# Two of seven mixing products replaced by a second level of seven, over two pairs of token tiles

## The chip, the cores and the metric

The kernel runs on one core of a Trainium2 chip. The metric is the device time of one execution in microseconds: 230.19 us before the change, the median of 3 runs (229.83 to 230.55).

## The reference

One transformer block on 2048 tokens of width 512: linear attention, then a gated mixer whose spatial weight mixes all tokens. Random bf16 inputs; cut to what matters:

```python
x = A_x                                              # 1 x 2048 x 512
h = x + _A_ref(_layernorm(x), A_wqkv, A_wo)          # linear attention, 32 heads
h2 = h + _B_ref(_layernorm(h), B_w_in, B_w_sp, B_b_sp, B_w_out)

def _B_ref(x, w_in, w_sp, b_sp, w_out):              # F = 1792, Fh = 896
    z = _gelu(jnp.einsum('bsd,df->bsf', x, w_in))
    z1 = z[..., :Fh].copy()
    z2 = _layernorm(z[..., Fh:], axis=-1)
    g = jnp.einsum('ts,bsf->btf', w_sp, z2) + b_sp[None, :, None]
    return jnp.einsum('bsf,fd->bsd', z1 * g, w_out)
```

The change concerns the product of `w_sp` (2048 x 2048) with `z2` (2048 x 896).

## The kernel before

Tokens are cut into 16 tiles of 128. The stages follow one another and overlap at the edges: normalize x and transpose it; keys, queries and the linear attention; h and its normalized, transposed form `hnT`; the two halves of `w_in` (`z2`, normalized, and the gate partner `z1`); the mixing with `w_sp`; the output product with `w_out`.

From the `w_in` stage on, large products are done by Winograd's form of the Strassen scheme: each factor is cut in 2 x 2 blocks, and seven products of blocks and some block sums take the place of eight products. One such unit for `w_in` is a *cell* (two token tiles: `cell3` for z2, `cell2` for z1; each of its seven products is 2 matmuls of 128 x 448). One for `w_out` is `mo_pair` (L1048: products of 3 matmuls of 128 x 256, and two remainders of 512 columns).

The unit for the mixing is `mix(i, c)` (L995) on a *pair*: output tiles i and i + 8. `wt[n]` holds the transposed rows of `w_sp` for output tile n, 16 blocks of 128 x 128. The four weight blocks of a pair are `y11, y21` (the first and second eight blocks of `wt[i]`) and `y12, y22` (those of `wt[i+8]`); the blocks of z2 are the first and last eight token tiles by the columns 0 to 447 (`lo`) and 448 to 895 (`hi`). Each of the seven products is 8 matmuls of 128 x 448. Three PSUM banks hold the results: `A`, `B`, `E` (a set; pairs take turns at the sets 0, 1, 2 and 3, 4, 5; banks 6 and 7 belong to `cell2` and `mo_pair`). In order of the program text:

- m1 = y11 with z2 `lo` into A (L1002); ScalarE copies A to B (L1003)
- VectorE: `q1 = y12 + y22` (L1004); m5 = q1 with `zt1` into E (L1005)
- ScalarE takes E out into `p5` twice, with the bias (L1007)
- VectorE: `q2`, and two more row sums written in place over `y12` and `y11` (L1008 to 1010)
- m6 onto B, m2 onto A, copy of B to E, m3 onto E, m7 and m4 onto B (L1011 to 1020)
- after m2, m3, m7 and m4 VectorE adds, multiplies with z1 (`gate`, `gate_p`), and SyncE sends the gated tile through a transposing DMA into `zgT` (L1017, L1022), which `mo_pair` reads.

`zt1`, `zt2`, `zt4` are sums of z2 blocks made once (`t1_sums`, `t_sums`). The pairs come in the order `MIX = (0, 1, 2, 3, 7, 4, 5, 6)`. Four cells of z1 stand among the pairs (`Z1S`, L956, L1085): cells 2 and 6 after the first pair, 3 and 7 after the second.

What sets the order: each operation is recorded with the tiles that it reads and writes (`add`, L106). Dependences come from their addresses, for PSUM from whole banks (L73). `ORDER` (L16) is a packed list of operation numbers; taken engine by engine it is the fixed instruction order of each queue, and a wait is placed wherever an operation depends on another engine or a DMA (`emit`, L163). Nothing is reordered at run time, so an instruction that waits holds back all that stands behind it on its engine.

All weight tiles `wt` are loaded by transposing DMAs on SyncE's queue (`load_w`), two per tile. Tiles 4, 12, 5, 13, 6, 14 (`W4`, L1088) share memory with the sums `hs` and `ws` of the cells, so they can only be loaded when the last cell has read those.

`sa`, `p5`, `vs`, `us`, `tmp` are buffers for row sums, biased products and the sums of `mo_pair`; before the change `vs`, `us` and `tmp` lie where `hnT` was (`o_pk`), and a dummy matmul (L1090) orders them behind the last cell.

Of the kernel before, what the change touches and what calls it, by code (L numbers as in the profile page):

```python
# [6 lines left out]
FP32 = mybir.dt.float32  # L7
# [4 lines left out]
P = 128  # L12
GRAN = 16
EARLY = 0
SEM_NS = 45.0
ORDER = "c-jrpg8~@j0tV0z|7_c~ZQHhOw_44tc{SU%QA5qPS6j`h*4DPRd!ON)Scr|d0EqaAgXBmFBOQbkNRNObNQH<fh6pH%49JKyh=<}xi!4Zh)F^?HNQkT`g-j@ovdE0=sD*5(gSIG#D9C}j$c5UdhcZZnoG6d>$c+j}jQYrf{K$)TsE7{eh<s>(0;q&eXox~+jDo0)LFkM|Xo4h&jsX~mu4sxc&<s`41<g?fg)ta4&>ht<8A(wcU!ogoVj_B=1-`=9n1YsQg`PNqNf?4;n2KJQhC^71p@@nZ=#4)327NIdtuYL3FdWOV0wb^rt1%uwV<x`GNQ}Z^tid>}#X9uEFBpwkn1KG6gQNHX8!;Q3@GaJ31Lop5V&FT>!znDrd_=+`9K#qa!C0KYX)Hx#Y{nLx#2;9Ot$2uC*oNKMjy+g_g?NPhIDozQ5&Q5H&f*{*;|$JW2X^8-uHXVL;|4C`Dz4!YZXzb0;1;gqC7$9}+{P>1!9CnXWd4R|c!3RkjVSyR&#;DT`5YVh7veA~|3ggP$KQy{7<_<__y_A4oxdX<qwx(s{lCIHB;>zH%C~qAGZEu6Hk0u)K0u7c<Rk-=Fe0-v2MaI)3o-#CF(=EgBy%wp6SELgGdEK(9m}#5YcM5ivnJCs16MH(OS2A}GcEJ5F!M4qi?AH?u_(*46}xdIv#=O5F(d0TKP#{WTeBj2vO6oW7AvzQi?bf<vjlsv7ppNFzhoO`WdnZAZ}<;;^Dz5xJcsftwq;*7WOdGBI}YJ@Y|kp3z;F2@8?ghAa4vslKlbNrPUIX`<s>#`N6zCg4(BiYiEnv_T{xe&c#OAsh)3Cs$9b2(@*PKT0T=QFf8#+8;39TqW8ULQuIFOj=L25gQ@-a#PG%>b;w3)gM^53t9LdXU!p(fn!}`F^yuxI9LFfx!r9>syRQ|_N%%>z8%+VZ6>oX%LseWgEjbTbH;W$RrKt@tf3Kh^a{=rW?%~YDsmpsGNimX@~#2=VOv2~W26-C#$l-F5Ag%n3|^^gTsN`;k0Gx&;GHIvy?LQ%Dx#S~4=R8p_mTm#ia15{M;lwIf8RHap1W%WJNY8h9srM57>a;S_Rv4zU%F%zhjHnF^JFr5bJD^*u|B~%9GR0XwGbPds9-DDeeRz+=P4Sk_5%BAznsG9ndnY4|S^cUwVx4P<UeW_aNrbK$e;rd3qG*p#UTMM*P!!%cUG)i@}TYs~PMrwriXr9_CvEFdB_9}*AYC9LHyT)je7HS9Esje0)ua;<^R&%V{>zXEOsn)22Zm5T@>!zw|ijHWR#%ZeRsi$tKmu~Bw)@q&ZXuNi^nwIOJrs)^$VsG8mdfn3mb<}k2=C}G)^|e7W^qc<G3T@PPy01-Ypq2VwKj?S;p?|bloitNhG*Mf%hY$5YhxAx|v`UZkvsUYg`s$cY>ZqQopJu6{-U{BPy?m~He5MonsL$H27dox|Jgzf(ua}yw*E+xtqW7zjPN|6h(*>3AC!Ll2N`I=cF6x}@+Aiuj+M(dTRmcbQM*UUH#U06)bx9HYmm)isuPBCNI<^b@N1azmM|C{Maa>1n8ULjCPT)k2=!8z}22SGAj^?DU<4#WI<WA{wPT`uqs#N~P^<Bzoo!YgW#$|oPbsgR5T-hC*-WgrR8C>2KoXORk#T9+WSzXVKebAYm&4--bRbAaV+|ZqU!uNd49evVAeabm~#;4uLz1+mdoy&LK&0XBohyAm2`>b2JtGoN0&%1`d@d)?yNMG^=S8^Wbbu(XaK40`@_i<~t^)-L*fBe=xeAPpI)4%$<o4cJyxwqRmzkl<65A`iS@Ie3Juie7K{m66N*T4IrAA7X>`H7!-ko)_oUwD`c_y^DSbHDOS|LcN&=W%}R_a5vIUgy8v(qsIm2lz|3_eB5YkN#wY|NPkuF~e9-_ZObz%?=@Ah#daU6=r$7qlCC2LWmt^c&_7xSRqn~9-@T_jvqF8o)d?J;kIWwPFU{*AyG&YrZ{<+?1i4{ubeSt4oSl_rwrfvjW;-1ND~%0bx09Xg{)zXvxRgaeaIBPbIGvQ*+Y(yGc5KpZ*-Qh)wx5ikSEOd4lj59P%z{TMMB}Q(yN>=6bOaFHm`8;P&zDesj%G(yxLn_CKL;0L%Fcm4MX{`&pTZqR1OtGrBEdt@P6-djIi5P!wnY=)x%Qnam~;;Gz!(ikFF7#gxcXJ*9mn))KDv=4JAU;&@9vs^+JQtJoF4LLd(!Pv<iJfo6sw?4ShrV&@prgokP3OA!G=hLjTY`bPK)1fG{xh3tdBx@IT`6A!q"  # L16


class _Op:
# [233 lines left out]
def bass_sequential_preLN__linear_attn_block__mixer_gmlp__prompt_kernel(  # L253
# [30 lines left out]
    def take(n):  # L284
# [57 lines left out]
          for c, os in enumerate(((o_sp + 5 * ZR, o_win + KD * FH * 2), (o_win + KD * FH * 2 + S, o_win + KD * FH * 2 + 2 * S)))]  # L342
# [1 line left out]
    p5z = [g.sbuf(f"p5z{c}", o_wo + c * ZR, [HW], FP32) for c in (0, 1)]  # L344
    u_t = [g.sbuf(f"u{c}", o_sp + 4 * ZR + c * HW * 2, [HW], BF16) for c in (0, 1)]
    V3 = HF * D
    vs = [g.sbuf(f"vs{k}", o_pk + k * V3, [HF, D // 2], BF16) for k in range(4)]
    us = [[g.sbuf(f"us{c}{k}", o_pk + 4 * V3 + (4 * c + k) * HF * P * 2, [HF, P], BF16) for k in range(4)] for c in (0, 1)]
    tmp = [[g.sbuf(f"tmp{c}{k}", o_pk + 4 * V3 + 8 * HF * P * 2 + (2 * c + k) * 2 * D, [D // 2], FP32) for k in (0, 1)]
           for c in (0, 1)]  # L350
    wout = g.sbuf("wout", o_wout, [KF, D], BF16)
    ct = g.sbuf("ct", o_ct, [KD, D], BF16)
    m = g.sbuf("m", o_m, [KD, D], BF16)
# [51 lines left out]
    def matmuls(out_ap, pairs, start=True, stop=True, onto=False, **k):  # L405
        n = out_ap.free_size() if callable(getattr(out_ap, "free_size", None)) else out_ap.shape[-1]

        kw = {"skip_group_check": True} if onto else {}

        def fn(pe):  # L410
            inst = None
            for i, (a, b) in enumerate(pairs):
                inst = pe.matmul(out_ap, lhsT=a, rhs=b, start=start and i == 0, stop=stop and i == len(pairs) - 1, **kw)  # L413
            return inst
        return PE(fn, [a for p in pairs for a in p], [out_ap], len(pairs) * max(65.0, n / 2.4 + 2.5), **k)
# [7 lines left out]
    def act(out_ap, in_ap, func, n, bias=None, scale=None, extra=(), accum=None, **k):  # L423
        kw = {}
        if bias is not None:
            kw["bias"] = bias
        if scale is not None:
            kw["scale"] = scale
        if accum is not None:
            kw["accum_out"] = accum  # L430
        ps = in_ap.tensor.name == "psum"
        return g.add("ACT", lambda ac: ac.activation(out_ap, in_ap, func, **kw), [in_ap, *extra],  # L432
                     [out_ap] + ([accum] if accum is not None else []),
                     cost=act_cost(n, ps) + 93 * len(extra) + (92 if accum is not None else 0), lat=120, **k)
# [10 lines left out]
    def dma_t(out_ap, in_ap, name, issue=1310.0, lat=1600.0, **k):  # L445
        return g.add("SP", lambda q: q.dma_start_transpose(out_ap, in_ap), [in_ap], [out_ap], cost=issue, lat=lat,  # L446
                     dma=name, **k)
# [276 lines left out]
    def load_w(n):  # L724
        nonlocal late
        for j in (0, HT):
            op = dma_t(wt[n][:, j:j + HT, :], B_w_sp[n * P:(n + 1) * P, j * P:(j + HT) * P], f"wt{n}", issue=1350, lat=2900)
            op.soft.add(late.i)
            late = op
# [109 lines left out]
    def half(b):  # L839
        return bank(b, HW)  # L840
# [4 lines left out]
    def comb(out_ap, a, b, op):  # L845
        n = 1
        for s in out_ap.shape[1:]:
            n *= s
        return dve(lambda v: v.tensor_tensor(out_ap, a, b, op), [a, b], [out_ap], n, acc=2)  # L849
# [103 lines left out]

    SETS = (0, 3)
    Z1C = {1: (0,), 3: (1,), 5: (4,), 7: (5,)}
    Z1S = {0: (2, 6), 1: (3, 7)}  # L956
    HB = 2
    SQ = range(0, NT - 2, 2)
    w_sums(win2, wq1[1])
# [22 lines left out]
    def gate(n, c, b):  # L982
        o = z1[n][:, c]
        dve(lambda v: v.scalar_tensor_tensor(o, half(b), b32[:, n:n + 1], o, op0=ALU.add, op1=ALU.mult),  # L984
            [half(b), b32[:, n:n + 1], o], [o], HW, ps=True)
# [3 lines left out]
    def gate_p(n, c, b, p):  # L989
        o, u = z1[n][:, c], u_t[cnt[0] % 2]  # L990
        cnt[0] += 1
        dve(lambda v: v.tensor_tensor(u, half(b), p, ALU.add), [half(b), p], [u], HW, ps=True)  # L992
        dve(lambda v: v.tensor_tensor(o, u, o, ALU.mult), [u, o], [o], HW, acc=2)

    def mix(i, c):  # L995
        B, A, E = SETS[c], SETS[c] + 1, SETS[c] + 2
        tl, th = i, i + HT
        q1, q2 = sa[c]
        pa, pb = p5[c]
        y11, y21, y12, y22 = (wt[n][:, s:s + HT, :] for n in (tl, th) for s in (0, HT))  # L1000
        ss = range(HT)
        matmuls(half(A), [(wt[tl][:, s, :], z2[:, s, lo]) for s in ss])  # L1002
        copy(half(B), half(A))  # L1003
        comb(q1, y12, y22, ALU.add)  # L1004
        matmuls(half(E), [(q1[:, s, :], zt1[:, s, :]) for s in ss])  # L1005
        for t, p in ((tl, pa), (th, pb)):
            act(p, half(E), ACT.Identity, HW, bias=b32[:, t:t + 1], extra=[b32[:, t:t + 1]])  # L1007
        comb(q2, q1, y11, ALU.subtract)  # L1008
        comb(y12, y11, y12, ALU.subtract)
        comb(y11, y21, q2, ALU.subtract)  # L1010
        matmuls(half(B), [(q2[:, s, :], zt2[:, s, :]) for s in ss], **onto)  # L1011
        matmuls(half(A), [(wt[tl][:, HT + s, :], z2[:, HT + s, lo]) for s in ss], **onto)
        gate(tl, lo, A)
        copy(half(E), half(B))
        matmuls(half(E), [(wt[tl][:, s, :], z2[:, HT + s, hi]) for s in ss], **onto)
        gate_p(tl, hi, E, pa)
        dma_t(zgT[tl], z1[tl], f"zg{tl}", issue=1300, lat=1750)  # L1017
        matmuls(half(B), [(wt[th][:, s, :], z2[:, s, hi]) for s in ss], **onto)
        gate_p(th, hi, B, pb)
        matmuls(half(B), [(wt[th][:, HT + s, :], zt4[:, s, :]) for s in ss], **onto)  # L1020
        gate(th, lo, B)
        dma_t(zgT[th], z1[th], f"zg{th}", issue=1300, lat=1750)  # L1022


    DH2 = D // 2
# [54 lines left out]
    for n in W3:  # L1080
        load_w(n)
    MIX = (0, 1, 2, 3, 7, 4, 5, 6)
    for c, i in enumerate(MIX):
        mix(i, c % 2)
        for q in Z1S.get(c, ()):  # L1085
            cell2(q, win1, wq1[0], 6, 7, p5z[q % 2], z1_half)
        if c == max(Z1S):
            for n in W4:  # L1088
                load_w(n)
    PE(lambda pe: pe.matmul(bank(7), lhsT=hnT[:, 0, 0:P], rhs=wout[:, 0, :], start=True, stop=True), [hnT[:, 0, 0:P], wout[:, 0, :]],  # L1090
       [bank(7)], 216)
    wout_sums()
# [36 lines left out]
```

## Time and profile before

| | before |
|---|---|
| median of 3 runs | 230.19 us (229.83 to 230.55) |
| the profiled execution: its time, its span | 230.16 us, 228.4 us |
| TensorE busy (PE), matmuls | 221.4 us, 1253 |
| VectorE busy (DVE) | 177.8 us, 397 instructions |
| ScalarE busy (ACT) | 123.3 us, 232 instructions |
| GpSimd busy (POOL) | 49.7 us, 134 instructions |
| DMA moved | 26.85 MB |
| granted TensorE clock | 1.00 in every stretch |

How to read the profile: times are microseconds from the start of the span. PE is TensorE's matmuls and PEld its weight loads, which run beside them. A matmul's time from start to end is longer than the distance to the next one's start, since they are pipelined: where a row says x8, the step is found from the start of this row to the start of the next. The same is true of VectorE: a row's mean is some 0.08 us longer than the step from one start to the next. "L413" is the helper that emits nearly all matmuls, L432 the one for ScalarE, L849 the one for block sums on VectorE, L852 the adds in PSUM of the cells, L443 and L446 the ones for plain and transposing DMAs on SyncE (SPq). In names like `psum<-z,wt` the operand that is streamed comes first and the one that is loaded as weights second. "[0.53 <-DVE h L1077]" means that the engine sat idle for 0.53 us before this row, and what released it.

### The profile page before, as it was taken

To read this page: it belongs to the slowest core of one execution; us is meant where nothing else is said; L and a number is where in the kernel's file an instruction comes from. 1 tells how busy PE (TensorE), PEld (TensorE's weight loads), DVE (VectorE), ACT (ScalarE), POOL (GpSimd) and SP (SyncE) were. 2 spreads that over 40 slices of the span, in tenths; PEclk is the share of its full clock that TensorE was granted. 3 is DMA by queue.
4 is the path that set the end of the run, shared out by engine and by line. 5 is a ranking of instruction groups with operands and counts; after the bars stand their busy time and mean duration, and the time that the engine had idled before them with its cause. 6 is when DMAs were issued, how large, how long until landed. Compare 5 with 4: busy or idle time off the path is not lost.

```text
span 228.4 us, 3524 instructions
## 1 busy us (share of the span) xinstructions
PE 221.4 (97%) x1253; PEld 115.3 (50%) x1253; DVE 177.8 (78%) x397; ACT 123.3 (54%) x232; POOL 49.7 (22%) x134
## 2 busy tenths in 40 slices
PE   7999999999999998999999999999999999999995
PEld 7444444453344443544545455555655556655553
DVE  3999656689999998999999955638877677553973
ACT  5794663489999998998654234425202213222111
POOL 2533600000567735595800000000000000000000
DMA  7725439957463337799980291249893150170664
GB/s 216 244 49 138 71 72 324 257 112 181 100 134 68 69 72 93 147 184 198 228 121 0 40 109 20 42 81 148 188 193 64 43 108 19 28 78 0 149 160 153
DMA packets 73905, 26.85 MB, mean 118 GB/s; under 512 B 63648, under 2 KB 73888, under 8 KB 73888
## 3 DMA queue, kind: packets, MB, share of 16 engines
q1 hardware_dynamic: 73184, 26.03, 56.0%
q10 hardware_dynamic: 704, 0.59, 0.8%
q8 instruction: 10, 0.16, 0.4%
q14 instruction: 7, 0.06, 0.1%
HBM read 6.95 MB, written 2.10 MB: 40 GB/s over the span
## 4 chain that ended last, share of the span: by engine, by line
PE 63%; DVE 12%; DMA 7%; ACT 7%; SPq 6%; POOL 3%; issue 2%; DVEq 0%
PE psum L413 57%; SPq L446 6%; PE psum L670 4%; DMA hnT<-hn 2%; DMA wt<-in_B_w_sp_dram 2%; DMA xnT<-xn 2%; ACT z L432 1%; DMA x<-in_A_x_dram 1%; DVE st L929 1%; DVE h L1077 1%; DVE pqT L803 1%; DVE h L815 1%; ACT xn L432 1%; ACT sq L432 1%; DVE psum L852 1%
## 5 line engine op out<-in xcount | busy, mean ns | idle before, releaser
L432 ACT ACTIVATE psum<-psum 128x448 f32<-128x448 f32 (+1 forms) x49 | 22.1, 464 | 57.7 <-PE psum L413 35.7
L413 PE MATMUL psum<-z,wt 128*128 128x448 bf16 x256 | 53.0, 353 | 0.0
L413 PEld LDWEIGHTS psum<-z,wt 128*128 128x128 bf16 x256 | 24.8, 98 | 22.1 <-DVE wt L849 0.6
L413 PE MATMUL psum<-win,hnT 128*128 128x448 bf16 x112 | 26.0, 352 | 1.0 <-DMA hnT<-hn 1.0
L413 PE MATMUL psum<-zt,sa 128*128 128x448 bf16 x128 | 26.7, 352 | 0.0
L432 ACT ACTIVATE z1t<-psum 128x448 bf16<-128x448 f32 (+1 forms) x24 | 16.1, 676 | 17.9 <-PE psum L413 17.2
L432 ACT ACTIVATE e<-psum 128x1024 bf16<-128x1024 f32 (+1 forms) x18 | 16.7, 927 | 13.1 <-PE psum L413 12.4
L852 DVE TENSOR_TENSOR psum<-psum,p5z 128x448 f32<-128x448 f32 x24 | 14.9, 624 | 5.8 <-ACT z1t L432 5.1
L413 PE MATMUL psum<-ws,hs 128*128 128x448 bf16 x72 | 18.9, 353 | 0.0
L413 PEld LDWEIGHTS psum<-zt,sa 128*128 128x128 bf16 x128 | 12.4, 98 | 11.0 <-DVE zt L849 0.4
L413 PEld LDWEIGHTS psum<-win,hnT 128*128 128x128 bf16 x112 | 10.8, 98 | 11.6 <-ACT z1t L432 1.7
L413 PE MATMUL psum<-wout,zgT 128*128 128x256 bf16 (+1 forms) x77 | 15.1, 302 | 0.8 <-DVE h L1077 0.7
L413 PE MATMUL psum<-xnT,wqkv 128*128 128x512 bf16 x64 | 15.5, 379 | 0.0
L984 DVE SCALAR_TENSOR_TENSOR z1t<-psum,b,z1t 128x448 bf16<-128x448 f32 x16 | 10.8, 682 | 5.8 <-PE psum L413 5.8
L413 PE MATMUL psum<-wqkv,xnT 128*128 128x512 bf16 x64 | 15.0, 379 | 0.2 <-DMA xnT<-xn 0.2
L432 ACT ACTIVATE z<-psum 128x896 bf16<-128x896 f32 x16 | 14.8, 944 | 0.6 <-PE psum L413 0.6
L670 PE MATMUL psum<-pk,xn 128*128 128x512 bf16 x64 | 15.1, 379 | 0.0
L413 PE MATMUL psum<-m,pqT 128*128 128x512 bf16 x64 | 14.6, 380 | 0.2 <-DVE h L815 0.2
L992 DVE TENSOR_TENSOR u<-psum,p 128x448 bf16<-128x448 f32 x16 | 9.9, 623 | 5.2 <-PE psum L413 5.1
L545 POOL TENSOR_SCALAR st<-st 128x1 f32<-128x1 f32 x10 | 4.2, 419 | 44.5 <-ACT sh L432 35.2
L592 DVE TENSOR_SCALAR e<-e 128x1024 bf16<-128x1024 bf16 (+1 forms) x18 | 7.2, 400 | 8.3 <-ACT e L432 8.1
L413 PE MATMUL psum<-zt,wt 128*128 128x448 bf16 x64 | 13.4, 352 | 0.0
(124 smaller groups left out, 384.4 us busy)
## 6 DMA issues: line engine op xcount, KB each, us to landing
r<-rcp SPq DMA_DIRECT2D x16, 128.0 KB, 2.7
out_dram<-h SPq DMA_DIRECT2D x15, 128.0 KB, 2.0
win<-in_B_w_in_dram SPq DMA_DIRECT2D x2, 896.0 KB, 8.8
x<-in_A_x_dram SPq DMA_DIRECT2D x6, 256.0 KB, 3.6
wqkv<-in_A_wqkv_dram SPq DMA_DIRECT2D x2, 512.0 KB, 4.4
wout<-in_B_w_out_dram SPq DMA_DIRECT2D x1, 896.0 KB, 6.5
wo<-in_A_wo_dram SPq DMA_DIRECT2D x1, 512.0 KB, 5.4
wt<-in_B_w_sp_dram SPq DMA_TRANSPOSE x32, 4.2
```

The lines of the kernel that those rows point to most:

```text
L413: inst = pe.matmul(out_ap, lhsT=a, rhs=b, start=start and i == 0, stop=stop and i == len(pairs) - 1, **kw)
L432: return g.add("ACT", lambda ac: ac.activation(out_ap, in_ap, func, **kw), [in_ap, *extra], [out_ap] + ([accum] if accum is not None else []),
L446: return g.add("SP", lambda q: q.dma_start_transpose(out_ap, in_ap), [in_ap], [out_ap], cost=issue, lat=lat, dma=name, **k)
L545: pool(lambda p: p.tensor_scalar(s[:, 2:3], s[:, 0:1], s[:, 0:1], -1.0 / (n * n), op0=ALU.mult, op1=ALU.mult), [s[:, 0:1]], [s[:, 2:3]], 240)
L592: dve(lambda v: v.tensor_scalar(e, e, 1.0, EPS_PHI, op0=ALU.min, op1=ALU.add), [e], [e], w * GW, acc=4)
L670: inst = pe.matmul(bank(CB[c]), lhsT=xn[:, i, c * P:(c + 1) * P], rhs=pk[:, i, :], start=i == 0, stop=i == NT - 1)
L803: dve(lambda v, q=q, r=r: v.tensor_tensor(q, q, r, ALU.mult), [q, r], [q], 2 * GW, acc=2)
L815: dve(lambda v, n=n, b=b, s=s: v.scalar_tensor_tensor(h[:, n, :], bank(b), 1.0, x[:, n, :], op0=ALU.mult, op1=ALU.add, accum_out=s[:, 0:1] ...
L852: dve(lambda v: v.tensor_tensor(half(b), half(src), p, ALU.add), [half(src), p], [half(b)], HW, ps=True)
L929: dve(lambda v, c=c, k=k: v.bn_stats(s[:, 6 * k:6 * k + 6], z2[:, n, c]), [z2[:, n, c]], [s[:, 6 * k:6 * k + 6]], HW)
L984: dve(lambda v: v.scalar_tensor_tensor(o, half(b), b32[:, n:n + 1], o, op0=ALU.add, op1=ALU.mult), [half(b), b32[:, n:n + 1], o], [o], HW, ...
L992: dve(lambda v: v.tensor_tensor(u, half(b), p, ALU.add), [half(b), p], [u], HW, ps=True)
```

## The change

`mix` now takes two pairs at once, a group: (0,1), (2,3), (7,4), (5,6). In the last three groups (`NEST = (0, 3, 3, 3)`: bit 1 for m1, bit 2 for m5) the products m1 of both pairs, which share the factor z2 `lo`, are done as one product of a two by two block matrix: the two pairs are the rows, each factor is halved again (4 of the 8 blocks of tokens, 224 of the 448 columns), and seven products of 4 matmuls of 128 x 224 take the place of 2 x 8 matmuls of 128 x 448. The same is done for m5 with `zt1`. Each of these nested products (`nested`) adds four row sums on VectorE (`nu1`, `nu5`), four copies between banks on ScalarE and two adds in PSUM on VectorE. The sums of the z2 side (`nv1`, `nv5`, four each) are made once by `quarter_sums`. The other five products of each pair stay as they were.

```diff
-    Z1S = {0: (2, 6), 1: (3, 7)}
+    ZLATE = (2, 6, 3, 7)
+    NEST = (0, 3, 3, 3)
...
+    HQ, H4 = HW // 2, HT // 2
+
+    def quarter_sums(v, z):
+        y11, y12, y21, y22 = (z[:, k:k + H4, f:f + HQ] for k in (0, H4) for f in (0, HQ))
+        comb(v[0], y12, y11, ALU.subtract)
+        comb(v[1], y22, v[0], ALU.subtract)
+        comb(v[2], y22, y12, ALU.subtract)
+        comb(v[3], y21, v[1], ALU.subtract)
+
+    def nested(X, Y, xa, xb, z, u, v, p):
+        X0, X1, Y0, Y1 = (bank(q, HQ, f) for q in (X, Y) for f in (0, HQ))
+        r11, r12, r21, r22 = (x_[:, k:k + H4, :] for x_ in (xa, xb) for k in (0, H4))
+        comb(u[0], r21, r22, ALU.add)
+        comb(u[1], u[0], r11, ALU.subtract)
+        comb(u[2], r11, r21, ALU.subtract)
+        comb(u[3], r12, u[1], ALU.subtract)
+        ks = range(H4)
+        prod = lambda o, x_, y_, **k: matmuls(o, [(x_[:, s, :], y_[:, s, :]) for s in ks], **k)
+        add = lambda o: dve(lambda e: e.tensor_tensor(o, o, p, ALU.add), [o, p], [o], HQ, ps=True)
+        copy = lambda o, i: act(o, i, ACT.Copy, HQ)
+        prod(X0, r11, z[:, 0:H4, 0:HQ])
+        prod(X1, u[0], v[0], **onto)
+        copy(Y1, X0)
+        copy(p, X1)
+        prod(X0, r12, z[:, H4:HT, 0:HQ], **onto)
+        prod(Y1, u[1], v[1], **onto)
+        copy(X1, Y1)
+        prod(Y1, u[2], v[2], **onto)
+        copy(Y0, Y1)
+        add(Y1)
+        prod(X1, u[3], z[:, H4:HT, HQ:HW], **onto)
+        add(X1)
+        prod(Y0, r22, v[3], **onto)
...
+        if nest & 1:
+            nested(SETS[0] + 1, SETS[1] + 1, wt[ia][:, 0:HT, :], wt[ib][:, 0:HT, :], z2[:, 0:HT, lo], nu1, nv1, np1)
+        for i, c in sets:
...
+            if not nest & 1:
+                matmuls(half(A), [(wt[i][:, s, :], z2[:, s, lo]) for s in ss])
+            copy(half(B), half(A))
+            comb(sa[c][0], y12, y22, ALU.add)
+            comb(sa[c][1], sa[c][0], y11, ALU.subtract)
+            if not nest & 2:
+                q1 = sa[c][0]
+                matmuls(half(E), [(q1[:, s, :], zt1[:, s, :]) for s in ss])
+        if nest & 2:
+            nested(SETS[0] + 2, SETS[1] + 2, sa[0][0], sa[1][0], zt1, nu5, nv5, np5)
...
+    for k in range(0, HT, 2):
+        mix(MIX[k], MIX[k + 1], NEST[k // 2])
+        if k == 0:
+            for q in ZLATE:
+                cell2(q, win1, wq1[0], 6, 7, p5z[q % 2], z1_half)
             for n in W4:
                 load_w(n)
+            if any(m & 1 for m in NEST):
+                quarter_sums(nv1, z2[:, 0:HT, lo])
+            if any(m & 2 for m in NEST):
+                quarter_sums(nv5, zt1)
```

The new sums need memory: `vs` and half of `us` move into the parts of the `wt` slots 0, 1, 8 and 9 that `zgT` leaves free, and the `nv` and `nu` buffers lie where `hnT`, the z1 half of `w_in`, `wo` and two smaller buffers were. So they can be written only after the cells have read those.

`ORDER` is replaced by a new list, for all engines and from the start of the program. Read as queues, the parts that matter later:

- SyncE, early: before, the transposes of token tiles 15 and 14 of the normalized x, then the loads of `wv`, `wo`, `win2`, `win1`. After: tile 15, `wv`, `wo`, `win2`, tile 14, `win1`. ScalarE's norm of tile 14 comes one exp later than before.
- SyncE, late: zgT0, wt7, zgT1, wt7, zgT8, zgT9, wt15 (two), the loads of wt4, wt12, wt5, wt13, wt6, then zgT10, zgT2, zgT3, then wt14. Before, the two loads of wt13 and all of wt6 and wt14 came after zgT10 and zgT2.
- VectorE, early: the sums `ws` of both `w_in` halves are all made ahead of the last query products' work; before, three of them were made some 40 to 85 operations later. From there up to the cell's add at 107.65 us the queue keeps nearly the same operations in the same places.
- TensorE: the four late cells stand among the products of pairs 0 and 1 and the first products of group (2,3). There the queue reads (N1, N5: nested m1, m5):

```
cell 7 m1, N1 X0, cell 7 m5, pair 1 m4, cell 7 m2, N1 X1, cell 7 m6, N5 X0, N5 X1, cell 7 m3, cell 7 m7,
N1 X0+, N5 X0+, cell 7 m4, N1 Y1+, mo_pair(0), N5 Y1+, N1 X1+, mo_pair(0), N5 X1+, N1 Y1+, N5 Y1+,
pair 2 m2, N1 Y0+, pair 2 m6, ...
```

- VectorE in that stretch: cell 7's first add, `nv5[1]`, `us00`, `nv1[1]`, cell 7's second add, `nu1[1]`, `nu1[2]`, `nu5[1]`, `nu1[3]`, `nu5[3]`, `nv1[2]`, then the first add of N1.

## Prediction

> **What bounds the kernel now.** I read the page first (busy shares, slices, the chain that ended last), then the merged chain in order of time, then TensorE's timeline from 104 us on, and last a table of busy time by stage.
>
> ```profile
> span 228.4 us, 3524 instructions
> ...
> PE 221.4 (97%) x1253; PEld 115.3 (50%) x1253; DVE 177.8 (78%) x397; ACT 123.3 (54%) x232; POOL 49.7 (22%) x134
> ...
> PE 63%; DVE 12%; DMA 7%; ACT 7%; SPq 6%; POOL 3%; issue 2%; DVEq 0%
> ```
>
> ```profile
> 104.54 45.53 PE psum L413 x238
> ...
> 163.26 4.32 DMA wt<-in_B_w_sp_dram
> ...
> 168.96 0.60 DVE wt L849
> ...
> 170.55 45.35 PE psum L413 x277
> ```
>
> TensorE has work in nearly every slice, and from 104.54 us on the chain is TensorE's own product stream, broken once around 163 to 170 us by the late loads of the mixing weights. Removing products in that stretch should therefore move the end. How much is read from matmul steps (start to start), not from "busy", because matmuls overlap:
>
> ```profile
> 183.02 3.19 PE L413 MATMUL psum<-z,wt 128*128 128x448 bf16 x16
> 186.05 0.49 PE L413 MATMUL psum<-vs,us 128*128 128x256 bf16 x3
> 186.38 0.49 PE L413 MATMUL psum<-wout,zgT 128*128 128x256 bf16 x3
> 186.70 1.68 PE L413 MATMUL psum<-z,wt 128*128 128x448 bf16 x8
> ```
>
> Sixteen matmuls of 448 columns take 186.05 - 183.02 = 3.03 us, 189.4 ns each. Six of 256 take 0.65 us, 108.3 ns each. Sixteen of 512 take 3.45 us in the chain (at 36.76), 216 ns each.
>
> Check of the method: from 104.54 us the queue holds 512 matmuls of 448 columns (448 of the mixing, 64 of cells), 161 of 256 and 22 of 512: 96.97 + 17.44 + 4.75 = 119.2 us. The stream really ends at 225.5 us, so 121.0 us: only 1.8 us of stalls in all.
>
> **What the change takes off TensorE.** A replaced product over two pairs was 2 x 8 matmuls of 448 columns, 3.03 us. It becomes 7 x 4 = 28 matmuls of 224 columns, a size the trace lacks. Bounds by rows: above, the 256-column step, 108.3 ns, and 28 x 108.3 = 3.03 us, no gain at all. Below, the sixteen 128-column matmuls of L753, whose row in the timeline lasts 1.06 us with 0.22 for the last one: (1.06 - 0.22) / 15 = 56 ns, each with its own weight load. On the line between these two, 224 columns cost 95.2 ns (224 is nearest to the 256 row, and the 448 and 512 rows lie on nearly the same slope). So 28 x 95.2 = 2.67 us, 0.364 us saved, six times: **-2.19 us**. One more bound: weight loads show 98 ns each; were they to run one after another they would set the step, 28 x 98 = 2.74, and -1.7 us. L753's 56 ns step speaks against that.
>
> The Trainium skill, "TensorE: Matmul & The Clock Gate", section "Back-to-back issue gap", speaks against the change: it gives about 81 ns per matmul at 128 columns and 131 ns at 512 for a sustained stream with weight loads. By a straight line that is an estimate of 123 ns at 448 and 94 at 224: 16 x 123 = 1.96 us against 28 x 94 = 2.62, so each nested product would lose 0.66 us, +4 us in all. This trace shows 189 and 216 ns in the stream itself, so I do not use it. Its section on LDWEIGHTS gives columns / 1.2, an estimate of 107 ns for 128; as a floor under the step it would leave a gain of about 0.2 us in all. L753's step contradicts that floor.
>
> **What it adds.** Per nested product: 4 sums of 128x512 on VectorE (the hs rows of that size follow one another by 0.33 us), 2 adds in PSUM of 224 columns (between 0.34 us for 256 columns and something smaller; 0.30) and 4 copies of 224 columns on ScalarE (256 columns: 0.37). Six times: VectorE 7.9 + 3.6, ScalarE 24 x 0.37 = 8.9 us. Once: 8 quarter sums of 128x896, 0.54 us apart, 4.3 us. VectorE gains 15.8 us of work. From 104.5 to 225.7 it is busy 88.9 of 121.2 us and ScalarE 39.8, so both have room in sum. The place matters:
>
> ```profile
> 120.00:128.00 8.00, 8.00 (x44) 3.97 (x42) 8.00 (x16) 2.67 (x5) 0.00 (x0) 1.00 0.00 0
> 128.00:136.00 8.00, 8.00 (x44) 4.16 (x43) 6.18 (x13) 2.65 (x6) 0.00 (x0) 1.00 0.72 91
> 136.00:144.00 8.00, 8.00 (x44) 4.06 (x42) 4.72 (x10) 3.83 (x8) 0.00 (x0) 1.00 0.27 53
> 144.00:152.00 8.00, 8.00 (x45) 4.13 (x43) 2.68 (x5) 2.88 (x6) 0.00 (x0) 1.00 0.08 17
> ```
>
> (Columns after the length: PE, PEld, DVE, ACT, POOL, clock, DMA.) VectorE, third, is full until 128 us and then has slack. The new order puts nested group (2,3) at 134 to 146 us by summed steps, so its sums fall right after the full stretch. I walked VectorE's new queue with the steps above, from its add (line 852) at 107.65 us on, which both orders share.
>
> *The first nested group.* From that add to TensorE's 138 us the new queue holds 30.1 us of VectorE steps, the old one 27.3 (the difference is mainly three row sums, two quarter sums and `vs0`); now VectorE idles 0.93 + 0.89 + 2.02 us between 132 and 138 us. So it arrives just in step with TensorE instead of 3 us ahead. Two waits come out: the cell's add (m6, add, m3) has 0.76 us of nested products as cover and needs about 0.9 (0.54 to 0.62 and two hand-overs), 0.15 us late; behind that add stand `nv5_1`, `us00`, `nv1_1`, the next add and `u1`, 0.54 + 0.27 + 0.54 + 0.54 + 0.33 = 2.2 us, so `u1` is ready near 140.9 and its product is due at 140.7, 0.25 us late. **+0.4 us**; from 0 to 2.0, the latter if VectorE comes 1.6 us later than reckoned. Behind a waiting sum stand the adds of the last cell and the gates of pairs 0 and 1; the latter are waited for by their transposes.
>
> *The later nested groups.* Every hop (product, copy, product; product, copy, add, product) spans 0.4 to 5 us of other products. The tightest is the add before the last product of group (5,6) at 198 us, 0.2 us of slack. **+0.2 us**, 0 to 0.8. ScalarE's copies lie beside these products; its queue is a third full.
>
> *W4 loads.* They wait for the last cell's third sum. Its last reader ends near 149.6 us in the old queue by summed steps, and near 139.4 in the new one. zgT9 and the loads of wt15 stand in front until about 141.5, so SyncE starts W4 8.6 us earlier. Pair 4's `r21 + r22` (needed near 150.8) then has wt4 from about 147. The last load, wt14, now stands behind zgT10, zgT2 and zgT3 and lands near 172.6; its sum is reached at 175.3 us. So the break at 163 to 170 goes:
>
> ```profile
> 170.55 0.50 PE L413 MATMUL psum<-wout,zgT 128*128 128x256 bf16 x3 [0.53 <-DVE h L1077]
> ```
>
> Summed steps put that product at 169.59, so 0.96 us of stalls had gathered by then. What is late next is VectorE itself. **-0.7 us**, 0 to -1.0.
>
> *The tail.* zgT6 and zgT14 issue about 3.1 us ahead of their products; these transposes land 2.9 us after issue (minimum and median), 4.5 at most. 0, up to +0.5. The earlier `wout_sums` and the moved buffers lie in VectorE's slack; at worst they are in the 2.0 above.
>
> *The front, reordered on all queues.* VectorE's w_sums come sooner; in its full stretch 50 to 61 us one more sum (0.53 us) stands ahead, given back at 90 us. **+0.3 us**, from -0.7 (the 0.96 us wait for hnT at 89.1 us might go) to +0.6.
>
> Sum: -2.19 + 0.4 + 0.2 - 0.7 + 0.3 = **-2.0 us**. The profiled execution took 230.16 us (span 228.4, 1.8 around it), beside a median of 230.19. Forecast **228.2 us**.
>
> **Rivals.** (1) *The gain goes into hops.* VectorE is full from 105 to about 170 us, and the dependence is kept by whole PSUM bank, so each copy and add blocks both halves. With hop terms at 2.0 + 0.8: -2.19 + 2.8 - 0.7 + 0.3 = +0.2, **230.4 us**. For it: the full windows above. Against it: 10.4 us of idle VectorE between 128 and 152 us, and ScalarE idle most of that time. A 224-column step near 108 ns leads to the same place: 230.4.
>
> (2) *Slower: the transpose of token tile 14 lands late.* It was issued just ahead of four weight loads; now three of them stand before it in SyncE's queue.
>
> ```profile
> 32.87 0.58 SPq L443 DMA_DIRECT2D wqkv<-in_A_wqkv_dram  x1
> ...
> 35.15 12.21 SPq L446 DMA_TRANSPOSE wt<-in_B_w_sp_dram  x4
> ```
>
> The loads take 8.5 us from the first issue to the second-last landing (34.05 + 7.3 - 32.87), and a transpose behind loads waits: the slowest wt landing is 10.6 us. Tile 14's norm also moves behind an exp and ends near 35.1 us. If the loads start behind tile 15's transpose near 29 us, they end near 37.6 and tile 14 lands near 38.4; its product is due at 39.2. If they start at 32.9 as now, it lands near 42.2 and TensorE stalls 3 us: **231.2 us**. It costs from a landing after 39.2 us on, and turns the sign after 41.2. Against it: ScalarE and GpSimd have tile 15 ready near 27 us.
>
> (3) *The nested step is set by weight loads*, 98 ns: gain 1.7 us, **228.7**.
>
> **Chances.** The forecast with rival 3 (226.6 to 229.4): 0.70. Rival 1: 0.16. Rival 2 and like stalls: 0.14. The forecast's own bounds add up to 226.3 and beyond 230; all ends at once is unlikely, so I take 226.6, and 230.6 to take in most of rival 1. About 0.3% is what a measurement of this kernel can tell: faster 0.70, same 0.16, slower 0.14.
>
> **What would show it.** Nested matmuls 95 ns apart (108: no gain); TensorE's waits for VectorE between 137 and 143 us near 0.4 us (2: rival 1); the W4 loads from about 141 us and no gap near 170; no gap at 39 us (rival 2). It is wrong if the mixing starts 1 us later than 104.5, or if VectorE stays full past 150 with TensorE waiting.

## The result, and the profile after

The changed kernel takes 227.59 us (median of 4 runs, 227.34 to 227.91), beside 230.2 us before: ratio 0.9883, 95% interval 0.9863 to 0.9902. The forecast was 228.2. In a second series (`after_again`) it took 227.27 us, ratio 0.9874 (0.9849 to 0.9900). Its profiled execution took 227.34 us, 2.82 less than the one of before.

The head of the page of the changed kernel, its busy shares and its chain of waits by engine:

```profile
span 225.6 us, 3738 instructions
...
PE 217.9 (97%) x1311; PEld 123.0 (54%) x1325; DVE 193.5 (86%) x441; ACT 130.8 (58%) x256; POOL 51.3 (23%) x134
...
PE 83%; DMA 6%; DVE 5%; ACT 3%; SPq 1%; issue 1%; ACTq 0%
```

TensorE lost 3.5 us of busy time; that is a little too much, since 14 of its matmuls left no record (1311 matmuls beside 1325 weight loads). VectorE gained 15.7 us (forecast 15.8). TensorE's share of the chain rose from 63% to 83%: fewer stretches of other work set the end. The chain in order of time (start, length, what), from 67 us on:

```profile
67.18 66.08 PE psum L425 x343
133.28 0.68 DVE z1t L997
134.00 3.09 DMA zgT<-z1t
137.16 0.55 ACT z1t L444
137.74 0.64 DVE psum L864
138.43 0.57 PE psum L425 x2
139.02 0.55 ACT z1t L444
139.62 0.64 DVE psum L864
140.30 2.44 PE psum L425 x20
```

Between 67 and 104 us and at 163 to 170 us the chain of the kernel before passed through other engines and DMAs; those stretches are gone. One new place has come, at 133 to 140 us: the last cell of z1 (cell 7), whose adds TensorE waits for. TensorE's timeline there (start, length, columns, count, the wait in brackets):

```profile
137.68 0.55 PE L425 MATMUL psum<-nv,nu 128*128 128x224 bf16 x4
138.43 0.55 PE L425 MATMUL psum<-win,hs 128*128 128x448 bf16 x2 [0.20 <-DVE psum L864]
...
139.58 0.55 PE L425 MATMUL psum<-zt,sa 128*128 128x224 bf16 x4
140.30 0.55 PE L425 MATMUL psum<-ws,hnT 128*128 128x448 bf16 x2 [0.17 <-DVE psum L864]
140.76 0.56 PE L425 MATMUL psum<-nv,nu 128*128 128x224 bf16 x4
...
143.18 0.93 PE L425 MATMUL psum<-nv,nu 128*128 128x224 bf16 x8
143.94 1.68 PE L425 MATMUL psum<-z,wt 128*128 128x448 bf16 x8
```

Two things are read here. The last two rows give the step at 224 columns: eight matmuls in 143.94 - 143.18 = 0.76 us, 95 ns each. And four matmuls take 0.38 us, but 138.43 comes 0.75 us after 137.68, and 140.30 comes 0.72 after 139.58. So 0.37 and 0.34 us are lost; the brackets name only a part of each (a bracket counts from the modelled end of the last matmul, not from when the next could have started). Busy time by stage, same columns as in the prediction:

```profile
136.00:144.00 8.00, 7.57 (x63) 5.66 (x63) 7.80 (x19) 4.93 (x13) 0.00 (x0) 1.00 0.71 132
144.00:152.00 8.00, 8.00 (x54) 4.92 (x52) 8.00 (x19) 2.89 (x7) 0.00 (x0) 1.00 1.00 185
```

VectorE, at 4.72 and 2.68 us of 8 in these stages before, is at 7.80 and 8.00 now.

### The profile page after: what moved, and what is told of

Its sections match the earlier page's. It is cut to its first block, busy times and chain, and to the rows that moved or that the text cites. A ratio compares the mean times of both kernels' runs of the same rounds, so it can differ in the third digit from the quotient of the medians.

```text
span 225.6 us, 3738 instructions
## 1 busy us (share of the span) xinstructions
PE 217.9 (97%) x1311; PEld 123.0 (54%) x1325; DVE 193.5 (86%) x441; ACT 130.8 (58%) x256; POOL 51.3 (23%) x134
## 4 chain that ended last, share of the span: by engine, by line
PE 83%; DMA 6%; DVE 5%; ACT 3%; SPq 1%; issue 1%; ACTq 0%
PE psum L425 75%; PE psum L682 6%; DMA x<-in_A_x_dram 3%; DMA r<-rcp 2%; DMA zgT<-z1t 1%; DVE st L533 1%; DVE h L1139 1%; ACT ct L444 1%; ACT e L444 1%; SPq L790 1%; DVE z1t L997 1%; DVE pqT L815 1%; DVE psum L864 1%; SPq L455 1%; ACT z1t L444 0%
## 5 line engine op out<-in xcount | busy, mean ns | idle before, releaser
L444 ACT ACTIVATE psum<-psum 128x448 f32<-128x448 f32 (+2 forms) x67 | 28.5, 436 | 48.0 <-PE psum L425 40.8
L425 PE MATMUL psum<-z,wt 128*128 128x448 bf16 (+1 forms) x232 | 46.2, 343 | 0.0
L425 PEld LDWEIGHTS psum<-z,wt 128*128 128x128 bf16 x232 | 22.7, 98 | 17.3
L425 PE MATMUL psum<-zt,sa 128*128 128x448 bf16 (+1 forms) x116 | 21.7, 323 | 0.1
L425 PE MATMUL psum<-xnT,wqkv 128*128 128x512 bf16 x61 | 15.0, 379 | 0.2
L425 PEld LDWEIGHTS psum<-zt,sa 128*128 128x128 bf16 x116 | 11.3, 98 | 7.0
L533 DVE BATCH_NORM_STATS2 st<-x 128x6 f32<-128x512 bf16 x15 | 9.7, 680 | 4.1 <-DMA x<-in_A_x_dram 4.1
L425 PE MATMUL psum<-wout,zgT 128*128 128x256 bf16 (+1 forms) x71 | 13.0, 295 | 0.2 <-DVE h L1139 0.2
```

The lines of the kernel that those rows point to most:

```text
L533: dve(lambda v: v.bn_stats(s[:, 0:6], src[:, n, :]), [src[:, n, :]], [s[:, 0:6]], D)
```

## The experiments

All are edits of the changed kernel, unless said otherwise. "Order" edits move instructions within the fixed queue of one engine; operation numbers in parentheses.

**after_again** is the changed kernel once more. 

> The changed kernel once more, as the measure for the others of this group. Both theories: 227.6 us, beside 230.2 before; ratio 0.988.

Measured: 227.27 us (226.94 to 227.70). This is what the others are compared with.

**no_second_level: the order without the products**

```diff
-    NEST = (0, 3, 3, 3)
+    NEST = (0, 0, 0, 0)
```

> The changed kernel and its new order, with the second level switched off in all groups: 12 whole products of 8 x 448 columns stand at the places of the nested ones (the first and the third of each seven), and the row sums, quarter sums, copies and adds of the nested products are gone. Theory: the products cost 6 x 0.364 = 2.2 us more, the 0.75 us of waits between 137 and 143 us go, since whole products cover them: 227.6 + 2.2 - 0.75 = 229.0. The W4 loads stay early, so no gap at 163 to 170. Rival (the new order makes the gain, not the second level): 227.6 to 228.

Measured: 229.57 us, ratio to before 0.9978 (0.9959 to 0.9996). So the second level is worth 2.3 us and the new order by itself some 0.6 (0.1 to 0.9 by the interval); the rival falls. The time is 0.6 us over the expectation. Its trace has waits of its own that cover the difference: by matmul steps 0.36 us near 144.4 and 0.63 us near 172.7. Between 137 and 143 us TensorE waits for nothing.

**second_level_two: only the last two groups**

```diff
-    NEST = (0, 3, 3, 3)
+    NEST = (0, 0, 3, 3)
```

> The changed kernel with the second level in the last two groups only; group (2,3) has its four whole products back, the eight quarter sums stay where they are on VectorE. Theory: the group's second level gains 0.73 us of products and pays 0.75 us of waits between 137 and 143 us, so this is as fast as the changed kernel: 227.6 (227.3 to 227.9). Rival (the waits come from VectorE being full with quarter sums, not from the group's products being short): waits stay, and the time is 228.3.

Measured: 227.69 us, ratio 0.9894 (0.9868 to 0.9919), beside 227.27 for all three groups: by these medians, whose spreads overlap, the first group wins 0.4 us where its products alone are worth 0.73. The front starts at different times in different executions, so the traces are set against one shared product, the last of pair 0 (starting at 131.57 us in the changed kernel, 131.17 here). From there to the last output product's start near the end (221.57 and 221.38) it is 90.00 us with the first group and 90.21 without. By this the group wins 0.2 us. From 137 to 143 us TensorE waits for nothing here, so the waits there belong to the short products and not to the quarter sums, which still stand on VectorE. No wait is listed up to 216 us, but by steps 0.36 us are lost near 144.3, ahead of and behind the dummy matmul, as in no_second_level. So the group's 0.8 us of waits stand against 0.4 without it, which is why it wins anything at all.

**nested_128: what sets the step**

```diff
-        prod = lambda o, x_, y_, **k: matmuls(o, [(x_[:, s, :], y_[:, s, :]) for s in ks], **k)
+        prod = lambda o, x_, y_, **k: matmuls(o[:, 0:P], [(x_[:, s, :], y_[:, s, 0:P]) for s in ks], **k)
```

> The changed kernel with the nested products cut to 128 of their 224 columns (the other 96 columns of each quarter are left out); all sums, copies and adds stay. Theory (columns set the step, on the line from 56 ns at 128 to 108 at 256): nested matmuls 56 ns apart, PE has 168 x 39 ns = 6.6 us less work, part of which hand-overs with less cover take back: 221 to 224. Rival (3) of the prediction (weight loads of 98 ns set the step): still 95 to 98 ns apart, and 227.3.

Measured: 224.32 us in one execution. TensorE's timeline of this kernel:

```profile
140.23 0.39 PE L425 MATMUL psum<-z,wt 128*128 128x128 bf16 x4
140.46 0.39 PE L425 MATMUL psum<-zt,sa 128*128 128x128 bf16 x4
...
146.25 0.39 PE L425 MATMUL psum<-nv,wt 128*128 128x128 bf16 x4
146.47 1.68 PE L425 MATMUL psum<-zt,sa 128*128 128x448 bf16 x8
```

Four matmuls take 0.23 and 0.22 us, 55 to 58 ns each, all with new weights. The step follows the columns and the weight loads of 98 ns do not set it: rival (3) of the prediction is refuted. Only 3.0 of the 6.6 us of saved products show in the time (0.3 short of the expected range): with less cover the same hand-overs cost more, 1.2 us of waits for the cell's adds beside 0.4 listed in the changed kernel. Another 0.5 us is a later start: the query product that starts near 21 us starts at 21.85 here and at 21.33 there.

**w4_late: the W4 loads as late as before** (on top of no_second_level)

```diff
+    g.ops[811].deps.add(869)     # first W4 load waits for a product that ends at 149.4 us
     g.schedule()
```

> The kernel no_second_level with one wait added: the W4 loads of mixing weights start when a product ends that runs from 147.9 to 149.4 us, as late as in the kernel before (150 us), in place of 139.4. Theory (their early start is what removed the break at 163 to 170, 0.7 us): 229.6 + 0.7 = 230.3, with a break of TensorE for VectorE sums or wt between 160 and 176 us. Rival (the start doesn't matter, the break went for another reason): 229.6.

Measured: 229.80 us beside 229.57, ratio to before 0.9977 (0.9954 to 0.9999). SyncE's timeline, then the waits (engine, line, releaser: total, count, longest) from 150 to 178 us:

```profile
149.63 2.58 SPq L458 DMA_TRANSPOSE wt<-in_B_w_sp_dram  x2
```

```profile
DVE sa L861 <- DMA wt<-in_B_w_sp_dram: 3.9, 1, 3.9
```

The loads start at 149.6 us, as in the kernel before (150.1), VectorE stands 3.9 us for one of them, and TensorE doesn't notice. The rival is right here: the early start by itself buys nothing in this order. The run tests the start alone: the loads up to wt6 still issue in one row, until 163.7 us, without the two transposes that stood among them in the kernel before.

**front_alone: before, with the new front (first try).** Each engine's queue of the kernel before, with its part ahead of the first mixing instruction taken from the changed kernel.

```diff
 every queue of the kernel before
-  the part ahead of its first mixing instruction, as in before
+  the same part as in the changed kernel
   the rest, as in before
```

> The kernel before with only the changed kernel's order of the front (all that each engine does ahead of its first mixing instruction); the mixing is as before. Theory (the front gained, because the 0.96 us wait for hnT and the stalls of 0.45 us ahead of 104.5 us went and a wait of 1.0 us for pqT came): 230.0 us, 0.2 under before. The prediction's step (front +0.3): 230.5. Rival (the whole gain beyond 2.2 us is the front's): 229.8 or less.

Measured: 238.53 us, and the front is not the cause. TensorE's waits for the cells' adds (total, count, longest):

```profile
PE psum L413 <- DVE psum L852: 5.1, 3, 3.0
```

The engines reach their first mixing instruction at very different times, so the cut put VectorE on one order and TensorE on the other from some 60 us on. The longest wait costs more than its length: TensorE starts nothing from 105.53 to 108.89 us, then the granted clock is 0.50 up to 111.9 us, and matmuls of 448 columns follow one another by 373 ns, some 1.5 us more. This run says nothing of the front.

**front_alone_2: the same, joined by time**

```diff
 every queue of the kernel before
-  the instructions shared up to the last cell3, as in before
+  the instructions shared up to the last cell3, as in the changed kernel
   the mixing instructions, as in before, put between by planned time
```

> The kernel before with the front in the changed kernel's order, second try: every instruction that both kernels share up to the last cell of the first kind stands in the changed kernel's order on its engine, the mixing instructions of before are put between them by the time at which each is planned. Theory: the front gains 0.2 us, 230.0. The prediction's step: 230.5. Rival (whole gain beyond 2.2 us is the front's): 229.8 or less. If the mixing, being ordered for another front, waits by itself, the trace is read at the first product of the last cell's second half only.

Measured: 230.14 us, ratio 0.9987 (0.9965 to 1.0008): no change that can be told. The trace says more than the time. The break at 163 to 170 us is gone here too, with the W4 loads at 150.18 us. VectorE's timeline, of the kernel before and then of this one (the wait in brackets):

```profile
167.60 0.69 DVE L849 TENSOR_TENSOR sa<-wt 128x1024 bf16<-128x1024 bf16 x1 [0.68 <-DMA wt<-in_B_w_sp_dram]
```

```profile
167.05 0.69 DVE L849 TENSOR_TENSOR sa<-wt 128x1024 bf16<-128x1024 bf16 x1
```

It is the same sum. Before, its load landed 0.68 us after VectorE came to it, and the output adds queued behind it came late to TensorE. Here the second half of the W4 loads is issued at 161.53 us, before at 161.91, and the load lands in time. It landed at 167.58 us before (163.26 + 4.32 in the chain) and at 167.05 or sooner here. So 0.7 us hung on half a microsecond in one landing, 0.4 of it from SyncE's queue.

**rcp_first: one swap on ScalarE**

```diff
 ScalarE's queue, 55 to 58 us
   r   <- psum,  third query group     (283)
+  rcp <- r,     third query group     (284)
   e   <- psum,  last query unit       (260)
-  rcp <- r,     third query group     (284)
```

> The changed kernel with one swap in ScalarE's queue: the reciprocal (rcp) of the third query group is made ahead of the exponential (e) of the last one, as in the kernel before. Theory (the wait of 1.0 us for pqT at 65.2 us comes from this order: the copies of rcp start 1.0 us later than they could): the wait falls to 0.1 to 0.5 us and the time to 226.6 (226.3 to 226.9). Rival (the fourth group's exponential is then 0.5 us later and the wait moves there): 227.3.

Measured: 226.66 us, ratio 0.9848 (0.9825 to 0.9871), the lowest median of all. The wait for pqT, in the changed kernel and then in this one:

```profile
65.23 3.63 PE L425 MATMUL psum<-m,pqT 128*128 128x512 bf16 x15 [1.04 <-DVE pqT L815]
```

```profile
64.87 3.41 PE L425 MATMUL psum<-m,pqT 128*128 128x512 bf16 x14 [0.27 <-DVE pqT L815]
```

Of the 0.8 us taken from the wait, 0.6 arrive at the end by the medians; within the traces, from the query product near 21 us to the last output product, it is 0.5 (200.24 and 199.74 us). The change had brought this wait in: before, rcp stood ahead of the exponential.

**cell_fix, both_fixes, rcp_and_cell, rcp_and_cell_2: cover for the last cell**

```diff
-    p5z = [g.sbuf(f"p5z{c}", o_wo + c * ZR, [HW], FP32) for c in (0, 1)]
+    p5z = [g.sbuf(f"p5z{c}", o_wo + c * (KD * D * 2 - ZR), [HW], FP32) for c in (0, 1)]
 cell_fix and both_fixes also:
-    enumerate((o_n + 4 * N4, o_n + 4 * N4 + S // 2, o_st3))
+    enumerate((o_n + 4 * N4, o_st3, o_n + 4 * N4 + S // 2))
 VectorE's queue (cell_fix)
+  nv1_1, u1 of the first product (824, 832)
   first add of cell 7 (803)
   nv5_1 (828)
+  u1 of the second product (855)
   second add of cell 7 (807)
 TensorE's queue (cell_fix): nested products 839, then 840 and 863,
 moved ahead of the cell's products 804 and 809
```

`both_fixes` adds the swap of rcp_first. `rcp_and_cell` leaves 803 in its place (824, 832 and 828 behind it) and moves only 840 and 863; `rcp_and_cell_2` moves only 840. Both have that swap too, and one copy (841) moved ahead on ScalarE.

> The changed kernel with the waits between 137 and 143 us covered: two buffers change places (p5z of the last cell no longer lies on the sums u0 and u1 of the first product's second level; the second sum of the other product lies on the old statistics), so both u1 sums and the quarter sums they meet stand ahead of the last cell's adds on VectorE, and three nested products are moved between the cell's products on TensorE as cover. Theory (0.75 us of waits are hand-overs of the last cell, product, gelu, add, product, with too little between): 0.2 us of waits are left and the time is 226.8 (226.6 to 227.0). Rival (VectorE is full there, and what is taken from the cell's adds is given back in the u sums after 141 us): 227.3.

> Both of the edits above. Theory: they add, 227.3 - 0.7 - 0.5 = 226.1 (225.8 to 226.5). Rival (one of them only moves its wait): 226.6 to 226.8.

> The changed kernel with the swap of rcp_first and a smaller edit at the last cell: p5z changes its place so that it no longer lies on u1, the second quarter sum of the first product and u1 are made between the cell's two adds, and only the u1 product (and one of the other nested product) is moved, ahead of and behind the cell's last product; the first add is not made to wait as in cell_fix. Theory (the second wait, 0.34 us near 140.3, lacks one product of cover; the first, 0.3 us near 138.4, is set by the landing of zgT8 and stays): 226.66 - 0.35 = 226.3 (226.1 to 226.5). Rival (VectorE has no room there, the u sums come late instead): 226.7 or more.

> rcp_and_cell with one mistake of it taken out: there the first sum u1 of the second product lies where the last cell's hnT is still read (the row of its nu sum after 0.65 us of waiting for TensorE), so its product could not be moved forward. Here that product stands behind the wout product again, and VectorE makes the last sum of the first product ahead of it. Theory (the waits at 137 to 143 us are the last cell's hand-overs plus a VectorE with hardly any room, so that only about 0.2 us can be won): the next mixing product of whole size starts 0.2 us earlier than in rcp_first against the same point of the front, and the time is 226.5 (226.2 to 226.7). Rival (VectorE is full and takes back all): 226.7 to 227.0.

Measured: 228.05 us for cell_fix, slower by 0.8 than the changed kernel; 227.10 for both_fixes, 227.23 for rcp_and_cell and 226.77 for rcp_and_cell_2, all no better than the swap alone (226.66). In cell_fix the two sums put ahead of 803 made the first add later: its product came at 139.23 us and not at 138.43. In cell_fix and both_fixes a wait of 0.58 us (by steps) for a ScalarE copy came as well, ahead of the product at 142.58 us in cell_fix: the copy stands behind two gelus of the cell. In rcp_and_cell the wait near 140.3 us did go, and a longer one came behind it, since u1 of the second product lies on memory that the cell's last product still reads. VectorE's timeline, then ScalarE's, both of rcp_and_cell:

```profile
140.66 0.43 DVE L861 TENSOR_TENSOR nu<-nu,sa 128x512 bf16<-128x512 bf16 x1 [0.65 <-PE psum L425]
```

```profile
136.86 0.55 ACT L444 ACTIVATE z1t<-psum 128x448 bf16<-128x448 f32 x1 [1.29 <-DMA zgT<-z1t]
```

The last row shows what makes the first add late: ScalarE's gelu writes z1 of token tile 14 into the slot of tile 8 and waits until the transposing DMA has read that out (zgT8, 3.09 us in the chain above). In rcp_and_cell_2, from the product ahead of the cell (133.13) to the whole product behind it (142.58), it is 9.45 us, beside 9.44 in rcp_first (134.28 to 143.72): nothing is won. All four expectations failed. The rival, that VectorE has no room there and takes back what is won, agrees with the times of the last two; it is not the only reason, as ScalarE's copy in the first two shows. A slot of its own for tile 14 wasn't tried, since the layout has no room for it.

## Why the prediction was right, step by step

The forecast was right in sign and size (-2.0 against -2.6 by the medians), but its terms are off in opposite ways, so part of the agreement in the sum is luck. The balance is made at TensorE's last output product, which starts at 224.22 us before and at 221.57 after, 2.65 us earlier. The front ends at the product that starts at 104.54 us before and at 103.95 us after, where one product of 0.38 us is still to be done that was done before. The first row is of the kernel before, the others of the changed one:

```profile
224.22 0.50 PE L413 MATMUL psum<-vs,zgT 128*128 128x256 bf16 x3
```

```profile
103.95 0.54 PE L425 MATMUL psum<-win,hs 128*128 128x448 bf16 x2
...
221.57 0.50 PE L425 MATMUL psum<-vs,zgT 128*128 128x256 bf16 x3
```

| step | forecast | found |
|---|---|---|
| products of 224 columns | -2.19 | -2.15 |
| first nested group | +0.4 | +0.8 |
| later nested groups | +0.2 | 0 |
| break at 163 to 170 us | -0.7 | -0.7 |
| front | +0.3 | -0.2 |
| small waits from 104 to 128 us, the tail | 0 | -0.4 |
| sum | -2.0 | -2.65 |

**Products: right.** The step is 95 to 96 ns (forecast 95.2); 28 x 95.5 = 2.67 us beside 3.03, six times 0.36. The Trainium skill, "TensorE: Matmul & The Clock Gate", section "Back-to-back issue gap", gives 81 ns per matmul for a sustained stream at 128 columns and calls columns / 2.4 + 2.5 ns the gap of an isolated matmul only. The stream here runs at the latter: an estimate by it of 55.8, 95.8 and 189.2 ns at 128, 224 and 448 columns stands beside 55 to 58, 95 to 96 and 189.4 measured.

**First nested group: place right, size and cause off.** From 134.65 to 143.94 us TensorE has one whole product, five cell products, eleven nested ones, two of three 256-column matmuls and one of 512: 1.52 + 1.89 + 4.20 + 0.65 + 0.22 = 8.48 us by steps. It takes 9.29: 0.8 us of waits. The prediction put the cell's add at 0.15 late and the u1 product at 0.25. The adds cost 0.37 and 0.34, the u1 product 0.08. The first has two parts. The product ahead of the add ends at 137.46 us and VectorE's sum ahead of it at 137.57, but the add starts at 137.74, behind the gelu that waited for zgT8 on the shared z1 slot. So an estimated 0.2 us belong to that landing, which the walk through VectorE's queue could not show, and what is left is about the 0.15 of the forecast. The second is a chain of product, gelu, add, product with 1.87 us from 138.43 to 140.30, of which 1.53 are covered (two cell products and two nested ones); the prediction had counted only one such chain. The forecast that VectorE comes "just in step" held: nothing that was moved there helped. With the second level the group wins about 0.2 us of its 0.73.

**Later nested groups: 0, not 0.2.** From 144 to 215 us no wait of TensorE is listed, and its matmuls follow one another by their steps (five gaps of 0.22 us there are each the place of one 512-column matmul that left no record).

**Break at 163 to 170: the effect right, the reason half right.** The loads start at 141.0 us (forecast 141.5; two of wt15 from 138.34 us stand ahead, 1.31 us each) and the 0.68 us are gone. But w4_late and front_alone_2 show that the early start was not needed: the break was one load that landed 0.68 us late at the head of VectorE's queue, and a landing half a microsecond sooner was enough in front_alone_2. Other shifts of the order could have taken this term too; that it came out to the tenth is partly luck.

**Front: wrong sign, and not settled to better than 0.3 us.** The prediction allowed -0.7 to +0.6. From the query product that starts near 21 us (21.04 before, 21.33 after) to the end of the front the changed kernel is 0.5 us faster. The wait of 0.96 us for hnT at 89 us went, as one end of the range had it, and the 0.45 us ahead of 104.54 too; the wait of 1.04 us for pqT came, which the prediction did not see, though ScalarE's order was to be read. rcp_first shows most of it to be the swap of rcp and exponential, worth 0.5 to 0.6 us. The 0.3 us at the start are no effect of the change that can be told: that product starts between 20.43 and 22.15 us in the thirteen kernels here that share the front up to it. front_alone_2 (from it to the first m5 product of the mixing 0.2 us slower than before, with a wait of 0.5 us near 81 us that the joining made) agrees within this.

**Small waits and tail.** From 104.54 to 127.96 us the kernel before took 0.3 us more than its steps, the changed one none over the same stretch; behind 215 us the waits add up to 0.7 us before and 0.6 after. The forecast had left this out.

**The rivals.** (1) Hand-overs eating the gain: they cost 0.8 us and not the 2.8 of that case; but for the first group alone the rival is nearly right. (2) The late transpose of token tile 14: issued at 35.37 us, it landed 3.0 us later, at 38.4 as the prediction reckoned for the harmless case; no wait of TensorE at 39 us, the products from 37.04 to 40.49 us stand without a gap over 0.05 us. (3) Weight loads: refuted by nested_128.

## What to carry to other kernels

- Price a product by its step from start to start at the size in question; between two sizes of one trace the line held to 1%. Then look, group by group, at what the shorter products used to cover: here two groups brought their full gain and the one beside the last cell a quarter of it.
- A wait whose releaser was only a few tenths late is worth its length to any edit that moves the queue a little. Before crediting it to one cause, undo that cause alone.
- When an order is replaced as a whole, read every queue for instructions that changed places around a long transfer. One swap of two ScalarE instructions was worth about a quarter of what the products gained.

## What the runs showed of the hardware

- Matmuls with new weights each time step by columns down to 128: 55 to 58 ns at 128, 95 to 96 at 224, 108 at 256, 189 at 448, 216 at 512, though each weight load is shown as 98 ns.
- The start of an execution varies by more than some terms of a forecast: the same product of the same front started between 20.43 and 22.15 us in thirteen executions, one of each kernel. Terms below half a microsecond are better read between two products of one trace than from whole times.
- A wait of TensorE of 3.4 us between two starts was followed by 3 us at a granted clock of 0.50 (front_alone, 108.9 to 111.9 us), while after one of 2.3 us in the same trace (89.39 to 91.69) the clock stayed at 1.00.
